# Strassen products in more layers of an attention-and-MoE kernel, under an order fixed in advance

## The chip, the cores and the metric

The kernel runs on one core of a Trainium2 chip. The metric is the device time of one execution in microseconds (us), as a median over runs. The profile is one further look at one execution; its span is some 2 us shorter than that execution's time.

**Work** of TensorE is the number of its matmuls times the time of one in an undisturbed sequence: 215.9 ns for 512 columns, 109 ns for 256, 56 ns for 128, 30.2 ns for 65. **Lag** at a moment is the time since the start of the span minus the work done until then, so a rise of the lag is time that TensorE lost, whether it stood still or ran at a lower clock. A **group** is the tokens of one batch (512 of 576; the other 64 of each batch are gathered in group "r").

## The reference

```python
# q, k, v: (8 batches, 8 heads, 576 tokens, 64); w_in: (512, 2048); w_out: (2048, 512)
r = lambda x: np.maximum(x, 0.0)
phi = lambda x: concat([r(x) * cos_w, r(x) * sin_w])      # cos_w, sin_w by position
kv  = einsum('bhsf,bhsd->bhfd', phi(k), v);  z = sum(phi(k), axis=2)
x   = einsum('bhsf,bhfd->bhsd', phi(q), kv) / (einsum('bhsf,bhf->bhs', phi(q), z) + 1e-6)
h   = tokens_by_512(x) @ w_in                              # "layer 1", 4608 tokens
out = (h * cos(h)) @ w_out                                 # "layer 2"
```

## The kernel before

The kernel makes a list of operations, each with engines that may do it, durations, dependencies and buffer slots. A list scheduler (`Plan.run`) places them in time; the resulting order is then the program of each engine. At run time each engine goes through its part in that order: in a_w_nox, one of the runs below, ScalarE stood 5.30 us before a feature whose data were late, and TensorE waited 4.0 us for a copy that comes behind it.

```python
class Plan:
    def run(self, cold=0.0):
        ...
            t0, e0 = min((c[0], c[1]) for c in cand)       # the engine that can start earliest
            t, _, us, o, _ = min(
                (c for c in cand if c[1] == e0 and c[0] <= t0 + self.EPS),
                key=lambda c: (c[4] if e0 == "DMA" else 0.0, c[3].prio, c[0]))
        ...
```

Loads of q, k and v are issued by SyncE. From batch 2 on, q features pass through a DMA transpose (`qT`), and from batch 3 on x does too (`xT`); SyncE issues these as well, in the same stream. The transfers of the weights are issued by GpSimd; they turn 32 bits into 16 on the way (the eight pieces land as 512 KB each, while the 36.74 MB that the page counts as read from HBM hold q, k and v with 28.3 MB and the weights with 8.4 MB, which is 32 bits a number).

```python
    def load(b, name, half, hs=ALLH):
        ...
            nc.sync.dma_start(out=blocks(m, n)[:, hs], in_=five[:, hs])
        ...
    def q_trans_dma(b, t):
        nc.sync.dma_start_transpose(
            out=qT(b, t), in_=qps[b][:, t].rearrange("p h g d -> p (h g d)"))

    def moe1(key, g, js, cs, s0, s1):                      # plain layer 1
        x = xR if g == "r" else xts[g]
        ...
                nc.tensor.matmul(
                    ps[key][:, n, :], lhsT=w_in_sb[:, c, j * P:(j + 1) * P],
                    rhs=x[:, c, s0:s1], ...)

    NG = 4
    def weights(n):                                        # 0..3 are quarters of w_in, 4..7 of w_out
        g = n % NG
        ...
                    def issue(...):                        # a load of batch 1 waits for w_out piece 1
                        if first:
                            nc.gpsimd.tensor_copy(
                                out=raw[name][0:2, 0, 0, 0:1],
                                in_=w_out_sb[0:2, (NG - 3) * NJT // NG, 0:1])
                        load(b, name, half, hs)
```

All first layers are plain matmuls. The second layer is plain in group 0 and a Strassen product (7 of 8 block products, with sums of blocks by VectorE) in the other groups.

Of the kernel before, what the change touches and what calls it, by code (L numbers as in the profile page):

```python
# [14 lines left out]

class Slot:


    def __init__(self, ring, n=1):
        self.ring, self.left, self.end = ring, n, 0.0  # L20


def flat(x):
    return tuple(z for y in x for z in flat(y)) if isinstance(x, tuple) else (x,)


class Op:
    def __init__(self, alts, prio, fn, deps, lat, acq, rel, at):
        self.alts, self.prio, self.fn, self.deps, self.lat = alts, flat(prio), fn, deps, lat
        self.acq, self.rel, self.at, self.end = acq, rel, at, None  # L30


class Plan:


    SEM, EPS = 0.08, 0.1

    def __init__(self, rings):
        self.ops, self.free = [], {r: [0.0] * n for r, n in rings.items()}
# [6 lines left out]
    def run(self, cold=0.0):  # L46
        users, wait = {}, {}
        for o in self.ops:
            wait[o] = len(o.deps)
            for d in o.deps:  # L50
                users.setdefault(d, []).append(o)
        ready = [o for o in self.ops if not wait[o]]
        clock, order = {}, []
        while ready:
            cand = []
            for o in ready:
                t = max([o.at] + [d.end + d.lat for d in o.deps])
                if any(not self.free[s.ring] for s in o.acq):
                    continue
                for s in o.acq:  # L60
                    t = max(t, min(self.free[s.ring]))
                for e, us in o.alts.items():
                    cand.append((max(t, clock.get(e, 0.0)), e, us, o, t))
            if not cand:
                left = [(o.prio, o.alts, [s.ring for s in o.acq if not self.free[s.ring]],
                         [(d.prio, d.alts) for d in o.deps if d.end is None][:3])
                        for o in self.ops if o.end is None]
                raise RuntimeError("no operation can start: " + repr(left[:12]))
            t0, e0 = min((c[0], c[1]) for c in cand)
            t, _, us, o, _ = min(  # L70
                (c for c in cand if c[1] == e0 and c[0] <= t0 + self.EPS),
                key=lambda c: (c[4] if e0 == "DMA" else 0.0, c[3].prio, c[0]))
            if e0 == "PE" and t < cold:
                us *= 1.7
            for s in o.acq:
                self.free[s.ring].remove(min(self.free[s.ring]))
            o.end = t + us + (self.SEM if us else 0.0)
            clock[e0] = t + us
            for s in o.rel:
                s.left, s.end = s.left - 1, max(s.end, o.end)  # L80
                if not s.left:
                    self.free[s.ring].append(s.end)
            order.append((t, len(order), o, e0))
            ready.remove(o)
            for u in users.get(o, ()):
                wait[u] -= 1
                if not wait[u]:
                    ready.append(u)
        assert len(order) == len(self.ops)
        order.sort(key=lambda x: x[:2])  # L90
        return [(o, e) for _, _, o, e in order]
# [3 lines left out]
def kernel(  # L95
# [50 lines left out]
    WT = cpool.tile([P, 4, HJ, HM], F16, name="WT")  # L146
# [4 lines left out]
    kvzs, kps, qps, qTs, qTr, x16s, xts, gts, sms, osts, ps = ({} for _ in range(11))  # L151
    T, T1 = range(NT), range(NT + 1)
    HS = [slice(0, HB), slice(HB, H)]
    RING = {"m1": 4, "l2": 2, "at": 1}
# [20 lines left out]
    def feat(eng, b, name, t, g, hs=ALLH):  # L175
        dst = (kps if name == "k" else qps)[b][:, t, hs, g, :]
        src, sc = raw[name][:, hs, t, :], CS[:, b % 2, g, t:t + 1]
        if eng == "A":
            nc.scalar.activation(out=dst, in_=src, func=AF.Relu, scale=sc)  # L179
        else:  # L180
            (nc.vector if eng == "V" else nc.gpsimd).tensor_scalar(  # L181
                out=dst, in0=src, scalar1=0.0, scalar2=sc, op0=ALU.max, op1=ALU.mult)
# [10 lines left out]
    def q_tiles(b):  # L193
        qps[b] = apool.tile([P, NT + 1, H, 2, D], F16, name=f"qp{b}", tag="qp", bufs=1)

    def qT_tiles(b):
        qTs[b] = apool.tile([P, NT, H, P], F16, name=f"qT{b}", tag="qT", bufs=1)

    def qR_tiles(b):
        qTr[b] = apool.tile([P, H, P], F16, name=f"qR{b}", tag="qR", bufs=2)  # L200

    def qT(b, t):
        return qTs[b][:, t] if t < NT else qTr[b]
# [27 lines left out]

    def ratio(b, t, tile_, hbs):
        nb, h0 = len(hbs), hbs[0] * HB
        den = apool.tile([P, nb, HB], F32, name=f"den{b}_{t}", tag="den")
        nc.vector.tensor_scalar_add(out=den, in0=tile_[:, :, :, D], scalar1=1e-6)
        rec = apool.tile([P, nb, HB], F32, name=f"rec{b}_{t}", tag="rec")
        nc.vector.reciprocal(out=rec, in_=den)  # L237
        if hbs[0] == 0:
            x16s[(b, t)] = apool.tile([P, H, D], F16, name=f"x16{b}_{t}", tag="x16", bufs=4)
# [19 lines left out]

    def transposes(key, tag, srcs_, **kw):  # L260
# [4 lines left out]
    def q_src(b, t, h):  # L265
        return qps[b][:, t, h].rearrange("p g d -> p (g d)")

    def q_trans_dma(b, t):
        nc.sync.dma_start_transpose(  # L269
            out=qT(b, t), in_=qps[b][:, t].rearrange("p h g d -> p (h g d)"))  # L270
# [12 lines left out]

    def sin(key):
        ps[("ch", key)] = apool.tile([P, SM], F32, name="ch", tag="ch", bufs=4)
# [4 lines left out]
    def gate(key, dst):  # L290
        m = ps[key]
        nc.vector.tensor_tensor(  # L292
            out=dst, in0=m, in1=ps[("ch", key)].rearrange("p (j s) -> p j s", s=m.shape[2]),
            op=ALU.mult)
# [4 lines left out]
    def s_tiles(g):  # L299
        sms[g] = gpool.tile([P, 2, HJ, HT], F16, name=f"s{g}", tag="s")  # L300

    def sums(g, c, n):
# [3 lines left out]
        a12, s1, s2 = gv[:, 1, js, 0:HT], sms[g][:, 0, js], sms[g][:, 1, js]  # L306
        out, in0, in1, op = ((s1, a21, a22, ALU.add), (s2, s1, a11, ALU.subtract),
                             (a21, a11, a21, ALU.subtract), (a12, a12, s2, ALU.subtract))[n]
        nc.vector.tensor_tensor(out=out, in0=in0, in1=in1, op=op)  # L309

    def weight_sum(n):
        wv = w_out_sb.rearrange("p (j e) m -> p e j m", e=2)
        b11, b12 = wv[:, 0, :, 0:HM], wv[:, 0, :, HM:Dm]
        b21, b22 = wv[:, 1, :, 0:HM], wv[:, 1, :, HM:Dm]
        x, y = ((b12, b11), (b22, WT[:, 0]), (b22, b12), (b21, WT[:, 1]))[n]
        nc.vector.tensor_tensor(out=WT[:, n], in0=x, in1=y, op=ALU.subtract)

    def prod(g, n, c):
        gv = gts[g].rearrange("p (j e) s -> p e j s", e=2)
        sv, wv = sms[g], w_out_sb.rearrange("p (j e) m -> p e j m", e=2)  # L320
        lo, hi, ml, mh = slice(0, HT), slice(HT, SM), slice(0, HM), slice(HM, Dm)
        bank, first, lhs, rhs = (
            ("X", True, gv[:, 0, :, lo], wv[:, 0, :, ml]),
            ("Y", True, sv[:, 1], WT[:, 1]),
            ("X", False, gv[:, 1, :, lo], wv[:, 1, :, ml]),
            ("Y", False, gv[:, 0, :, hi], WT[:, 2]),
            ("Z", True, sv[:, 0], WT[:, 0]),
# [469 lines left out]
```

## Time and profile before

| | before |
|---|---|
| median time when the change was predicted | 303.42 us (302.2 to 306.28, 3 runs) |
| span of the profile | 298.7 us |
| work of TensorE, dummies of the start included | 270.1 us |
| mean granted clock | 0.99 |
| lag at 20, 70, 200 us | 8.9, 12.9, 23.5 us |
| tail after the last matmul | 4.7 us |

These lines of the page of the kernel before are the busy time of each engine, the busy tenths in 40 slices of 7.5 us (the clock row in tenths of full speed), and the engines' shares of the chain of work that ended last.

```profile
PE 280.1 (94%) x2565; PEld 201.3 (67%) x2565; DVE 233.7 (78%) x450; ACT 175.6 (59%) x303; POOL 102.0 (34%) x107
PE   8879999899969987999979999999999999999993
DVE  1878888899995798887869798987786786768661
PEclk9979999999999999999999999999999999999998
DMA  7799995897899999999999999715202100200213
PE 55%; DMA 16%; DVE 10%; POOL 5%; SPq 5%; ACT 4%; issue 3%; ACTq 0%; DVEq 0%
```

TensorE bounds the kernel. From 203 us to 292 us it has no gap, and the DMA row has fallen off by then. Earlier, DMA is near full, and here TensorE has its stops. The view of what TensorE waited for (total us, times, longest) begins so; the timeline of TensorE has the longest stop in the middle, at 89.91 us (start, duration, engine, operation, and in brackets the idle time and what ended it).

```profile
PE N L228 <- DVE x L241: 2.8, 2, 2.1
PE M L279 <- ACT xT L159: 2.6, 1, 2.6
PE PY L337 <- DVE s L309: 2.2, 2, 1.6
```

```profile
89.91 3.61 PE L279 MATMUL M<-xT,w_in_sb 128*128 128x512 f16 x16 [2.60 <-ACT xT L159]
```

From 13 us on, when the real work begins, no stop lasts longer than 2.6 us.

### The profile page before, as it was taken

What the parts mean: (1) busy time and instruction counts of PE and PEld (TensorE: products, weight loads), DVE (VectorE), ACT (ScalarE), POOL (GpSimd) and SP (SyncE); (2) the same over time, 40 slices, a digit from 0 to 9 for tenths busy, and PEclk for the clock granted to TensorE, in tenths of its full rate; (3) what the DMA queues carried; (4) which work ended last, traced back from release to release, by engine and by line L of the source; (5) the groups of instructions that cost most, each with busy time, mean ns of one, the idle gap of its engine ahead of it and who ended that gap; (6) DMA issues with size and microseconds to landing.
All of it is one profiled execution on the core that took longest, in us unless ns stands there. A gap on an engine that the chain in (4) does not pass through costs nothing.

```text
span 298.7 us, 6583 instructions
## 1 busy us (share of the span) xinstructions
PE 280.1 (94%) x2565; PEld 201.3 (67%) x2565; DVE 233.7 (78%) x450; ACT 175.6 (59%) x303; POOL 102.0 (34%) x107
## 2 busy tenths in 40 slices
PE   8879999899969987999979999999999999999993
PEld 8768856688855555566646666776666666566782
DVE  1878888899995798887869798987786786768661
ACT  2846748599379797679489497634433443443210
POOL 1370004396191686287077194011002001100500
PEclk9979999999999999999999999999999999999998
DMA  7799995897899999999999999715202100200213
GB/s 218 264 163 203 204 362 183 279 308 120 273 274 235 356 232 169 283 278 203 322 256 202 238 369 195 141 47 151 35 0 94 48 1 32 111 2 0 91 52 140
DMA packets 77086, 53.29 MB, mean 178 GB/s; under 512 B 46080, under 2 KB 74752, under 8 KB 77056
## 3 DMA queue, kind: packets, MB, share of 16 engines
q1 hardware_dynamic: 69760, 39.73, 55.2%
q0 software_dynamic: 6848, 12.59, 16.6%
q10 hardware_dynamic: 448, 0.57, 0.5%
q8 instruction: 20, 0.33, 0.5%
q14 instruction: 10, 0.08, 0.1%
HBM read 36.74 MB, written 9.44 MB: 155 GB/s over the span
## 4 chain that ended last, share of the span: by engine, by line
PE 55%; DMA 16%; DVE 10%; POOL 5%; SPq 5%; ACT 4%; issue 3%; ACTq 0%; DVEq 0%
PE M L279 26%; DMA vm<-in_v_dram 13%; PE PY L337 8%; PE PZ L337 6%; PE PX L337 5%; PE M L376 5%; POOL qp L181 4%; DMA qm<-in_q_dram 3%; PE KV L219 2%; DVE g L292 2%; SPq L171 2%; DVE x L241 2%; PE TP L263 2%; DVE s L309 2%; SPq L269 1%
## 5 line engine op out<-in xcount | busy, mean ns | idle before, releaser
L279 PE MATMUL M<-xT,w_in_sb 128*128 128x512 f16 (+1 forms) x640 | 120.2, 336 | 2.9 <-ACT xT L159 2.6
L286 ACT ACTIVATE ch<-M 128x512 f32<-128x512 f32 x144 | 84.9, 595 | 60.8 <-PE M L279 58.7
L292 DVE TENSOR_TENSOR g<-M,ch 128x512 f16<-128x512 f32 x128 | 85.8, 687 | 27.0 <-ACT ch L286 26.1
L279 PEld LDWEIGHTS <-w_in_sb 128*128 128x128 f16 x704 | 67.3, 98 | 46.6 <-issue 3.1
L181 POOL TENSOR_SCALAR qp<-qm,CS 128x512 f16<-128x512 f32 x29 | 60.0, 2074 | 31.0 <-DMA qm<-in_q_dram 27.0
L337 PEld LDWEIGHTS <-g 128*128 128x128 f16 x560 | 54.1, 98 | 11.5
L369 POOL DMA_DIRECT2D out_dram<-ost x14 | 7.8, 558 | 98.6 <-DVE ost L351 42.5
L179 ACT ACTIVATE kp<-km,CS 128x512 f16<-128x512 f32 x52 | 35.1, 715 | 0.2
L179 ACT ACTIVATE qp<-qm,CS 128x512 f16<-128x512 f32 x40 | 26.9, 713 | 11.9 <-DMA qm<-in_q_dram 11.9
L337 PE MATMUL PX<-w_out_sb,g 128*128 128x256 f16 x224 | 27.6, 273 | 0.0
L241 DVE TENSOR_TENSOR x<-N,rec 128x512 f16<-128x512 f32 (+1 forms) x44 | 26.1, 594 | 1.7 <-DVE rec L237 0.2
L337 PE MATMUL PY<-WT,g 128*128 128x256 f16 x224 | 27.2, 273 | 0.0
L337 PEld LDWEIGHTS <-s 128*128 128x128 f16 x224 | 21.4, 98 | 7.1 <-DVE s L309 2.8
L161 POOL CAST V<-vm 128x512 f16<-128x512 f32 (+1 forms) x22 | 13.9, 664 | 15.9 <-DMA vm<-in_v_dram 15.9
L228 PE MATMUL N<-kvz,qT 128*128 128x65 f16 x256 | 14.7, 196 | 2.3 <-DVE x L241 2.1
L228 PEld LDWEIGHTS <-qT 128*128 128x128 f16 x256 | 12.6, 100 | 6.1 <-issue 3.5
L337 PE MATMUL PY<-WT,s 128*128 128x256 f16 x112 | 14.1, 273 | 2.2 <-DVE s L309 2.2
L181 DVE TENSOR_SCALAR kp<-km,CS 128x512 f16<-128x512 f32 x28 | 15.5, 590 | 0.3 <-DMA km<-in_k_dram 0.2
L292 DVE TENSOR_TENSOR gr<-M,ch 128x512 f16<-128x512 f32 x16 | 10.9, 689 | 5.7 <-ACT ch L286 5.5
L219 PE MATMUL KV<-V,kp 128*128 128x65 f16 x320 | 12.9, 196 | 2.5 <-DVE kp L181 0.7
L279 PE MATMUL M<-xR,w_in_sb 128*128 128x512 f16 x64 | 15.1, 379 | 0.0
L219 PEld LDWEIGHTS <-kp 128*128 128x128 f16 x320 | 11.7, 99 | 4.7 <-issue 2.4
(70 smaller groups left out, 287.7 us busy)
## 6 DMA issues: line engine op xcount, KB each, us to landing
out_dram<-ost POOLq DMA_DIRECT2D x28, 256.0 KB, 4.1
qm<-in_q_dram SPq DMA_DIRECT2D x8, 640.0 KB, 5.3
km<-in_k_dram SPq DMA_DIRECT2D x8, 640.0 KB, 7.0
qm<-in_q_dram SPq DMA_DIRECT2D x8, 512.0 KB, 5.8
km<-in_k_dram SPq DMA_DIRECT2D x8, 512.0 KB, 8.8
vm<-in_v_dram SPq DMA_DIRECT2D x6, 640.0 KB, 8.1
vm<-in_v_dram SPq DMA_DIRECT2D x6, 512.0 KB, 8.9
w_in_sb<-in_moe_w_in_dram POOLq DMA_DIRECT2D x4, 512.0 KB, 9.0
```

Of the source, the lines that this page charges most:

```text
L161: (nc.vector if eng == "V" else nc.gpsimd).tensor_copy(out=out, in_=in_)
L179: nc.scalar.activation(out=dst, in_=src, func=AF.Relu, scale=sc)
L181: (nc.vector if eng == "V" else nc.gpsimd).tensor_scalar(out=dst, in0=src, scalar1=0.0, scalar2=sc, op0=ALU.max, op1=ALU.mult)
L219: nc.tensor.matmul(tile_[:, n, hh, :], lhsT=kps[b][:, t, h].rearrange("p g d -> p (g d)"), rhs=V1[:, t, h, :], start=(t == 0), stop=(t == NT))
L228: nc.tensor.matmul(tile_[:, n, hh, :], lhsT=qT(p, t)[:, h, :], rhs=kvzs[p][:, h, :], start=(i == 0), stop=(i == len(parts) - 1))
L241: nc.vector.tensor_tensor(out=dst, in0=tile_[:, :, :, 0:D], in1=rec.unsqueeze(3).broadcast_to((P, nb, HB, D)), op=ALU.mult)
L279: nc.tensor.matmul(ps[key][:, n, :], lhsT=w_in_sb[:, c, j * P:(j + 1) * P], rhs=x[:, c, s0:s1], start=(c == 0 and n == 0), stop=(c == NCT ...
L286: nc.scalar.activation(out=ps[("ch", key)], in_=ps[key].rearrange("p j s -> p (j s)"), func=AF.Sin, bias=math.pi / 2.0, scale=1.0)
L292: nc.vector.tensor_tensor(out=dst, in0=m, in1=ps[("ch", key)].rearrange("p (j s) -> p j s", s=m.shape[2]), op=ALU.mult)
L337: nc.tensor.matmul(ps[(g, bank)][:, i, :], lhsT=lhs[:, j, i * P:(i + 1) * P], rhs=rhs[:, j], start=(first and i == 0 and j == 0), stop=(j ...
L369: e0.dma_start(out=five[:, t0:t0 + 2, :], in_=blocks(ost, n))
L376: nc.tensor.matmul(ps[("M2", t)], lhsT=gts[0][:, j, t * P:(t + 1) * P], rhs=w_out_sb[:, j, :], start=(j == 0), stop=(j == NJT - 1))
```

## The change

The intent is to save TensorE time with more Strassen products, and to win back the gaps of the middle with an order that was searched instead of scheduled greedily. Strassen is added in the second layer of group 0 and in the first layer of groups 6, r and 7: each takes 112 matmuls of 256 columns (12.2 us) in place of 64 of 512 (13.8 us). The order is a list of operation numbers with their engines. The operations in the text of the kernel still carry the durations of a model, in which loads and transposes form one queue and each lands a fixed 2.0 us (`LAND`) after it. The list scheduler of before uses the same kind of model. Buffers are smaller to make room for the sums of w_in. The weights' pieces go out as 0, 1, 5, 2, 4, 3, 7, 6 instead of 0 to 7, as the order says.

```diff
-    def run(self, cold=0.0):
-        ... (the list scheduler)
+    def run(self):
+        return [(self.ops[int(x.rstrip("VAG"))], x.lstrip("0123456789"))
+                for x in ORDER.split()]
+
+ORDER = """
+22 180 184 883 24 229 25 230 115 818 342 21 40V 41V 42A 60 44V 43A 46V 61A 62 47V 48A 66 63V 34A
+32V 39V 70 33A 31V 53G 54A 51V 30A 52G 38V 50G 35V 37A 36V 45A 49V 71 4G 64 72V 5G 55A 57V 75
+58A 68 76V 7G 56A 77V 85 59A 86V 15G 78 65A 87V 73 9G 74V 227 67A 95 90 96V 88 91V 13G 97V 79A
+92V 11G 80 98 69A 89V 93 105 19G 81V 82V 94A 116 99A 17G 106V 107V 83 100 120 84V 108 110 101V
 ... (72 more such lines; 5G to 19G are the weights' pieces)
-    WT = cpool.tile([P, 4, HJ, HM], F16, name="WT")
+    WT = cpool.tile([P, 3, HJ, HM], F16, name="WT")
+    WS = cpool.tile([P, 3, 2, HJ, P], F16, name="WS")
-    RING = {"m1": 4, "l2": 2, "at": 1}
+    RING = {"m1": 4, "l2": 2, "at": 1, "raw_k": 1, "raw_q": 1, "raw_v": 1, "kp": 1, "qp": 4,
+            "V1": 1, "kvz": 3, "qT": 4, "qR": 2, "xT": 2, "x16": 3, "ch": 3, "g": 2, "s": 3,
+            "ld": 16, "p5": 3, "xs": 1, "ost0": 1, "ost1": 1}
-        qps[b] = apool.tile([P, NT + 1, H, 2, D], F16, name=f"qp{b}", tag="qp", bufs=1)
+        qps[(b, t)] = apool.tile([P, H, 2, D], F16, name=f"qp{b}_{t}", tag="qp", bufs=RING["qp"])
+    def quad(g, qd, n):                                    # one Strassen product of layer 1
+        ...
+        bank, first, lhs, rhs = (
+            ("X", True, a11, x_block(g, 0, 0)), ("Z", True, ws[0], xs[0]),
+            ("Y", False, ws[1], xs[1]), ("X", False, a12, x_block(g, 1, 0)),
+            ("Y", False, s3, x_block(g, 0, 1)), ("Z", False, ws[2], x_block(g, 1, 1)),
+            ("Y", False, a22, xs[2]))[n]
+        ...
+    STR = {6, "r", 7}
 ...
-    def layer2_plain(base):
 ...
+    layer2(0, lambda i: (1, 1, i))                         # group 0's second layer: Strassen as well
 ...
         for o, e in plan.run():
-            if o.fn is not None:
-                o.fn(e) if e in ("A", "V", "G") else o.fn()
+            o.fn(e) if e else o.fn()
```

## The prediction

> **What bounds the kernel now.** TensorE. The page gives PE busy for 280 of 298.7 us, VectorE 78%, ScalarE 59%, GpSimd 34%, clock 0.99. [...] In the timeline, 4 matmuls of 512 columns follow each other in 0.865 us (216 ns each), 8 of 256 columns in 0.87 us (109 ns), 40 KV matmuls in 1.21 us, 8 numerator matmuls in 0.26 us. Times the counts this is about 264 us, besides the dummies of the start. Real work runs from 13.1 us to 294.0 us, so about 19 us of that stretch is lost: some 6 us before 23 us, 1-2 us near 55 us, 2.6 us at 87 us, 3 us at 110-115 us, 2.1 us at 152 us. From 203 us to 292 us TensorE has no gap at all; attention and its DMAs (DMA near full from 60 to 190 us in the slices) are over by then.
>
> **What the change does.** Group 0's second layer and the first layers of groups 6, r and 7 become Strassen: 112 matmuls of 109 ns for 64 of 216 ns, 12.2 for 13.8 us, so 1.6 us less each and 6.4 us in all. The weight loads (98 ns) still fit under 109 ns; second-layer Strassen shows that rate already. Two cover matmuls add 0.4 us. Of these 6 us, 4.8 us lie in the gap-free last stretch and count in full.
>
> The price is VectorE and ScalarE work. Per Strassen first layer: 8 additions (0.60 us apart when back to back) and 4 input sums; ScalarE 8 copies. The second layer gives back 2-3 VectorE adds per group: the first product seeds a PSUM bank. Counted in program order with the trace's durations, the last three groups hold 8.4-9.1 us VectorE and 4-7 us ScalarE work per 10 us of PE: tight, still under PE. The first 60 us of PE work, however, hold 64 us of VectorE work (57 before): sums of group 0 and of both weight matrices. There VectorE bounds: nothing gained, perhaps 1-3 us lost, before about 75 us.
>
> The middle is where the searched order may pay: some 8-9 us of PE gaps after 85 us come from late transposes, V loads and x copies. [...] a sum takes 0.68 us, up to 1.12 us; a K feature 0.48 us, up to 0.90 us. The change gives GpSimd 36 instead of 29 features[...]. I expect half of the middle gaps to go (4-5 us), as DMA stays full there. The tail (last matmul to end, 4.7 us) shortens by about 0.7 us.
>
> **Sum.** 298.7 - 6 (PE work) - 4.5 (gaps) - 0.7 (tail) + 1 (early VectorE) = about 288.5 us of span; the timed median lay 4.7 us above the profiled span before, of which I keep 2: 290.5 us. Range 283 to 298 us. Faster by over 2%: 0.85; within 2%: 0.13; slower: 0.02.
>
> **What would show it.** PE work 6 us less; the gap-free last stretch about 5 us shorter, without waits over 1 us; VectorE share up from 78% to 85-88%, ScalarE to about 66%; VectorE near 100% before 75 us; the chain of waits with more VectorE, less DMA.
>
> **What would make it wrong.** Strassen's alternating chain (copy, add, gate per quad) leaving PE waiting in the last groups, as VectorE is near 90%; or DMA-bound attention ending no earlier than 200 us, so only the last 5 us appear. Or the order removes nearly all gaps: about 282 us.

A matmul record of 512 columns (layer 1 from `xT`) lasts 379 ns in the mean in the kernel before, but in an undisturbed sequence the next one starts after 216 ns. The sum came to 288.5 us of span and 290.5 us of time.

## The result and the profile after

The changed kernel takes 319.6 us (318.79 to 320.27, 4 runs) beside 304.85 us (302.2 to 306.61, 4 runs) of the kernel before. It is slower by a ratio of 1.049, with a 95% interval of 1.0396 to 1.0585. Here and below, a ratio is the mean time of one kernel's fast runs over that of the kernel before in the same rounds, so it isn't quite the ratio of the medians quoted. Executions over 1.5% slower than the fastest of the same kernel are left out of the means. The profiled spans, 317.4 and 298.7 us, differ by more (18.7 us), because the profiled run of before was a fast one of its kind.

The page of the changed kernel, the lines that answer to those above:

```profile
PE 281.4 (89%) x2759; PEld 221.2 (70%) x2759; DVE 247.1 (78%) x465; ACT 194.1 (61%) x355; POOL 122.7 (39%) x121
PE   7779838977978997999899869999999999999993
DVE  1877956978978687688877957899889888798881
PEclk9989987999999999899999989999999999999998
DMA  7699992199997999399999979954502100110203
PE 50%; DMA 28%; DVE 6%; POOL 5%; ACT 4%; SPq 3%; issue 3%; ACTq 0%; DVEq 0%; POOLq 0%
```

TensorE's busy share fell from 94% to 89%, the DMA share of the chain rose from 16% to 28%, and the slices show a hole: slice 6 in PE, slices 6 and 7 in the clock, and slices 7 and 8 in DMA itself. (Slices are counted from 1; each is 7.9 us here.) The waits of TensorE begin now with a DMA, and the timeline has one stop of 5.15 us:

```profile
PE PX L436 <- DMA w_out_sb<-in_moe_w_out_dram: 5.2, 1, 5.2
PE M L325 <- DMA xT<-x: 4.2, 2, 2.7
PE N L262 <- ACT kvz L195: 2.7, 2, 1.6
PE M L325 <- ACT qp L215: 2.4, 1, 2.4
```

```profile
45.78 1.86 PE L436 MATMUL PX<-w_out_sb,g 128*128 128x256 f16 x8 [5.15 <-DMA w_out_sb<-in_moe_w_out_dram]
```

The work of TensorE is 264.0 us, 6.1 us less than before. Lag tells where the time went, by stretch of the span:

| lag, us | before | after | after loses more by |
|---|---|---|---|
| at 70 us | 12.9 | 24.9 | 12.0 |
| from 70 to 200 us | +10.6 | +19.5 | 8.9 |
| from 200 us to the last matmul | +0.4 | +4.2 | 3.8 |
| sum at the last matmul | 23.9 | 48.6 | 24.7 |

The sum fits: 24.7 us of lag more, less 6.1 us of work, are 18.6 of the 18.7 us of span. The last row but one is 23.9 - 23.5 and 48.6 - 44.4; a tail of 4.7 and 4.8 us comes after it.

A part of this is clock. The trace of the changed kernel has stretches at half clock from 20.9 us (3.4 us), 44.8 us (6.8 us), 126.7 us (3.4 us) and 188.1 us (3.4 us), 17.0 us in all beside 3.4 us before. TensorE did 7.8 us of work in them (1.4 us before). At half clock, matmuls of 256 columns start 213 ns apart in the median, beside 109 ns else, so each us of work there takes about one more us, and about 6.4 us of the 24.7 us go there. All these stretches last 3.41 or 6.83 us, and in the 3.41 us before the one at 44.8 us there is no matmul at all. What sets them off is not shown. (The list at the end has two stretches that came after shorter stops.) Windows of the trace (us busy on each engine, count, then clock, DMA share, GB/s), four us each around the stop:

```profile
44.00:48.00 4.00, 1.86 (x8) 1.14 (x8) 2.17 (x4) 0.32 (x1) 0.00 (x0) 0.59 1.09 364
48.00:52.00 4.00, 3.67 (x20) 2.71 (x20) 3.23 (x5) 1.04 (x3) 3.22 (x6) 0.55 0.34 112
```

In the second window TensorE is busy for 3.67 us, but makes only 20 matmuls of 256 columns, which is 2.2 us of work.

The cause of the stop itself can be read from SyncE's timeline: the first loads of batch 1, before and after.

```profile
33.88 0.60 SPq L171 DMA_DIRECT2D qm<-in_q_dram  x1
34.53 0.63 SPq L173 DMA_DIRECT2D qm<-in_q_dram  x1
35.28 0.96 SPq L171 DMA_DIRECT2D km<-in_k_dram  x1
```

```profile
27.42 0.60 SPq L207 DMA_DIRECT2D qm<-in_q_dram  x1
28.06 0.64 SPq L209 DMA_DIRECT2D qm<-in_q_dram  x1
28.80 0.60 SPq L207 DMA_DIRECT2D km<-in_k_dram  x1
29.45 4.88 SPq L209 DMA_DIRECT2D km<-in_k_dram  x1
34.43 4.50 SPq L207 DMA_DIRECT2D vm<-in_v_dram  x1
```

Batch 1's loads are held until piece 1 of w_out (number 5) has landed. Piece 5 now goes out third instead of sixth, so they start 6.5 us earlier, with five pieces issued behind that one instead of two; two of the issues then take 4.9 and 4.5 us, where one takes 0.6 us otherwise. The last piece of w_out landed at 45.8 us instead of 38.8 us. From issue to landing, min, median and max of w_out's pieces, before and after:

```profile
DMA to landing us min/median/max: 13.3/16.4/19.3
```

```profile
DMA to landing us min/median/max: 10.0/17.5/25.0
```

After 52 us there is nothing left to move for 8 us, and batch 2's q load goes out at 64.0 us instead of 51.4 us. That delay of 12.6 us does not simply stay: by batch 3 the q load is 7.9 us behind that of before and by batch 4 9.8 us, then 17.4 us at batch 5 and 22.5 us at batch 7. So there are two losses, one before batch 2 and one from batch 4 on.

### The profile page after: what moved, and what is told of

The parts are those of the page before. It is cut to its first block, busy times and chain, and to the rows that moved or that the text cites. A ratio compares the mean times of both kernels' runs of the same rounds, so it can differ in the third digit from the quotient of the medians.

```text
span 317.4 us, 7064 instructions
## 1 busy us (share of the span) xinstructions
PE 281.4 (89%) x2759; PEld 221.2 (70%) x2759; DVE 247.1 (78%) x465; ACT 194.1 (61%) x355; POOL 122.7 (39%) x121
## 4 chain that ended last, share of the span: by engine, by line
PE 50%; DMA 28%; DVE 6%; POOL 5%; ACT 4%; SPq 3%; issue 3%; ACTq 0%; DVEq 0%; POOLq 0%
PE M L325 11%; PE SD L436 9%; DMA km<-in_k_dram 9%; DMA w_out_sb<-in_moe_w_out_dram 9%; PE PZ L436 7%; PE PX L436 7%; DMA vm<-in_v_dram 6%; PE M L381 5%; PE SD L381 3%; PE YZ L381 3%; DMA qT<-qp 2%; POOL kp L217 2%; SPq L207 2%; PE PY L436 1%; PE KV L253 1%
## 5 line engine op out<-in xcount | busy, mean ns | idle before, releaser
L325 PE MATMUL M<-xT,w_in_sb 128*128 128x256 f16 (+1 forms) x512 | 94.4, 332 | 10.9 <-DMA xT<-x 4.2
L387 ACT ACTIVATE ch<-M 128x512 f32<-128x512 f32 x116 | 67.8, 595 | 45.4 <-PE M L325 30.3
L338 DVE TENSOR_TENSOR g<-M,ch 128x512 f16<-128x512 f32 x110 | 73.0, 685 | 16.7 <-ACT ch L387 15.9
L436 PEld LDWEIGHTS <-g 128*128 128x128 f16 x640 | 63.2, 100 | 22.1 <-issue 10.1
L217 POOL TENSOR_SCALAR qp<-qm,CS 128x512 f16<-128x512 f32 x19 | 39.8, 2100 | 34.0 <-DMA qm<-in_q_dram 32.3
L217 POOL TENSOR_SCALAR kp<-km,CS 128x512 f16<-128x512 f32 x17 | 38.5, 2271 | 9.6 <-DMA km<-in_k_dram 9.6
L215 ACT ACTIVATE qp<-qm,CS 128x512 f16<-128x512 f32 x43 | 29.6, 713 | 10.7 <-DMA qm<-in_q_dram 8.6
L215 ACT ACTIVATE kp<-km,CS 128x512 f16<-128x512 f32 x38 | 25.5, 713 | 3.7 <-DMA km<-in_k_dram 3.7
L381 PEld LDWEIGHTS <-w_in_sb 128*128 128x128 f16 x192 | 18.7, 98 | 2.9 <-issue 0.4
L436 PE MATMUL PZ<-w_out_sb,g 128*128 128x256 f16 x128 | 16.6, 273 | 0.5 <-DVE PZ L338 0.5
L217 DVE TENSOR_SCALAR kp<-km,CS 128x512 f16<-128x512 f32 x25 | 13.4, 568 | 4.5 <-DMA km<-in_k_dram 4.5
L436 PE MATMUL PZ<-WT,s 128*128 128x256 f16 x128 | 16.3, 273 | 0.0
L381 PEld LDWEIGHTS <-WS 128*128 128x128 f16 x144 | 14.0, 98 | 3.0 <-issue 1.2
L436 PE MATMUL SD<-WT,g 128*128 128x256 f16 x112 | 15.4, 283 | 0.6 <-ACT ost L195 0.6
## 6 DMA issues: line engine op xcount, KB each, us to landing
w_in_sb<-in_moe_w_in_dram POOLq DMA_DIRECT2D x4, 512.0 KB, 10.1
```

The lines of the kernel that those rows point to most:

```text
L215: nc.scalar.activation(out=dst, in_=src, func=AF.Relu, scale=sc)
L217: (nc.vector if eng == "V" else nc.gpsimd).tensor_scalar(out=dst, in0=src, scalar1=0.0, scalar2=sc, op0=ALU.max, op1=ALU.mult)
L325: nc.tensor.matmul(ps[key][:, n, :], lhsT=w_in_sb[:, c, j * P:(j + 1) * P], rhs=x[:, c, s0:s1], start=(c == 0 and n == 0), stop=(c == NCT ...
L338: (nc.vector if eng == "V" else nc.gpsimd).tensor_tensor(out=out, in0=in0, in1=in1, op=op)
L381: nc.tensor.matmul(ps[(g, qd, bank)][:, i, :], lhsT=lhs[:, c, 2 * qd + i, :], rhs=rhs[:, c, :], start=(first and i == 0 and c == 0), stop= ...
L387: nc.scalar.activation(out=ps[("ch", key)], in_=ps[key].rearrange("p j s -> p (j s)"), func=AF.Sin, bias=math.pi / 2.0, scale=1.0)
```

## The experiments

Eighteen kernels ran, in six jobs, each with three rounds beside the kernel before. The medians of before in these jobs are 304.11, 302.16, 304.07, 303.88, 303.1 and 302.63 us, on five different chips; so across jobs, differences of about 1% in a ratio, or 2 us, are not to be leaned on. "Old order of weights" below means pieces 0 to 7 in turn in the changed kernel. A kernel that is wrong is named so.

### Job 1: the start, and who made the order

**a_worder**: the changed kernel with the old order of weights. The tokens 15G, 9G, 11G, 19G, 17G become 9G, 11G, 15G, 17G, 19G (pieces 0 to 3 are 5G to 11G, pieces 4 to 7 are 13G to 19G); nothing else moves.

```diff
-58A 68 76V 7G 56A 77V 85 59A 86V 15G 78 65A 87V 73 9G 74V 227 67A 95 90 96V 88 91V 13G 97V 79A
-92V 11G 80 98 69A 89V 93 105 19G 81V 82V 94A 116 99A 17G 106V 107V 83 100 120 84V 108 110 101V
+58A 68 76V 7G 56A 77V 85 59A 86V 9G 78 65A 87V 73 11G 74V 227 67A 95 90 96V 88 91V 13G 97V 79A
+92V 15G 80 98 69A 89V 93 105 17G 81V 82V 94A 116 99A 19G 106V 107V 83 100 120 84V 108 110 101V
```

> Edit: the changed kernel with the eight weight transfers issued in the old order (four of w_in, then four of w_out), nothing else. Theory W (weights): the new order issues the second w_out piece third; the loads of batch 1, which wait for that piece, then start at 27.4 us instead of 33.9 us and take DMA time from the other weights, so that the last w_out piece lands at 45.8 us instead of 38.8 us; TensorE stops 5 us, its clock halves for 6.8 us, and everything of batch 2 comes some 12 us later. It expects w_out landed by 39-41 us, no TensorE stop over 1.5 us there, loads of batch 2 at 52-58 us instead of 64 us, and 304 to 312 us instead of 319.6. Rival V (VectorE overloaded before 75 us, as the prediction had it): the work of VectorE is the same, so 317 to 321 us and batch 2 as late as before.

Measured: 314.38 us, ratio 1.0323 (1.0244 to 1.0402), span 310.4 us. The long stop is gone, and the last piece takes at most 19.6 us to land. The gain is 5.2 us in the medians and 7.0 us in the span; the time missed the range that was expected, so the weights' order is a part of the loss and not most of it.

The lag at 70 us says the same: 21.2 us, beside 24.9 us in the changed kernel and 12.9 us before. Of the 12.0 us that were lost there, 3.7 us are back and 8.3 us are not. Where half of the rest lies can be read from TensorE's timeline. In the Strassen products of group 0's second layer there are five stops, 4.2 us in sum: on a piece of w_out, on a sum of w_out's blocks (`WT`), on a gated value (`g`), and on a copy and an addition between two products.

```profile
34.18 0.81 PE L436 MATMUL PX<-w_out_sb,g 128*128 128x256 f16 x6 [0.89 <-DMA w_out_sb<-in_moe_w_out_dram]
35.75 1.03 PE L436 MATMUL PY<-WT,s 128*128 128x256 f16 x8 [0.76 <-DVE WT L416]
42.07 0.83 PE L436 MATMUL PX<-w_out_sb,g 128*128 128x256 f16 x6 [1.36 <-DVE g L338]
43.59 1.91 PE L436 MATMUL PX<-w_out_sb,g 128*128 128x256 f16 x16 [0.69 <-ACT p L195]
49.53 1.03 PE L436 MATMUL PZ<-w_out_sb,g 128*128 128x256 f16 x8 [0.53 <-DVE PZ L338]
```

In the kernel before, whose second layer of group 0 is plain, the same view shows no stop from 28 to 55 us. No run undoes the Strassen product of group 0 alone, so this is read from traces and not tested.

**a_gate**: the new order of weights, but batch 1's loads wait for the piece of w_out with the last number, 7. (In the new order this is the last but one to be sent; piece 6 lands 2.5 us after it.)

```diff
-                                in_=w_out_sb[0:2, (NG - 3) * NJT // NG, 0:1])
+                                in_=w_out_sb[0:2, (NG - 1) * NJT // NG, 0:1])
```

> Edit: the changed kernel with its own weight order, but batch 1's loads wait for the last w_out piece instead of the second. Theory W, if the overlap of the two is what costs: w_out all landed by 38-40 us, batch 1's loads at 39-40 us and landed near 52-54 us, TensorE stop under 2 us, 308 to 315 us. If the order of the pieces itself were the cause and not the overlap: the fourth w_in piece still late, w_out late, 318 to 321 us. Rival V: 317 to 321 us.

Measured: 312.07 us, ratio 1.0252 (1.0175 to 1.033, so whether it is over 2% slower than before is unclear), span 310.5 us. With the new order of pieces kept, keeping the loads away from them gives back 7.5 us. The stop on w_out falls from 5.2 to 1.1 us. The lag at 70 us is 20.5 us. So it is the overlap of loads and weights that costs, not the order of the pieces as such.

**b_worder**: the kernel before, with the new order of the pieces (but for the last two, which are not swapped) and nothing else.

```diff
     def weights(n):
+        n = (0, 1, 5, 2, 4, 3, 6, 7)[n]
         g = n % NG
```

> Edit: the kernel before with the weights in the new order (w_in, w_in, w_out piece 2, w_in, w_out, w_in, w_out, w_out), nothing else. Theory W: batch 1's loads start near 27-28 us, the last w_out piece lands near 44-46 us, TensorE stops 3 to 6 us in the second layer of group 0, and the time grows by 4 to 12 us to 308 to 316 us. Rival V: no change over 1%, 303 to 307 us.

Measured: 312.25 us, ratio 1.0254 (1.0169 to 1.0339), span 310.9 us, 12.2 us longer than before. One line turns the old kernel into one that is 8 us slower. Its stop lies on w_in, since plain layer 1 needs those pieces when w_out's have overtaken them, and half clock follows it (from 33.4 us for 6.8 us). The wait of weight loads (PEld) in the trace:

```profile
PEld L279 <- DMA w_in_sb<-in_moe_w_in_dram: 7.6, 2, 5.2
```

**a_greedy**: all operations of the changed kernel, but ordered by the list scheduler of before instead of the fixed text.

```diff
-        return [(self.ops[int(x.rstrip("VAG"))], x.lstrip("0123456789"))
-                for x in ORDER.split()]
+        users, wait = {}, {}
+        ... (the list scheduler of the kernel before, with one line more for the engine name "Vp")
```

> Edit: all operations of the changed kernel (Strassen in the same layers, same buffers), ordered by the list scheduler of the kernel before in place of the fixed searched order. Theory W: the scheduler issues the weights in their plain order, so no late w_out; 295 to 308 us, clearly faster than the searched order. If the operations themselves (more VectorE and ScalarE work, chains of the Strassen quads) are the cause: 316 us or more.

Measured: 325.35 us, ratio 1.0682 (1.0584 to 1.0781). As a whole the searched order is better than greedy for these operations, so the theory that the order alone is the culprit was wrong. By stretches it is both better and worse. From 70 to 200 us the lag of a_greedy grows by 11.3 us, near the 10.6 us of before, where it grows by 19.5 us in the changed kernel and by 16.1 us in a_worder. After 200 us a_greedy loses 21.3 us, where the changed kernel loses 4.2 us. Its leading wait is that of TensorE on VectorE's additions between the products of a second layer (3.7 us in four stops).

### Job 2: buffers, VectorE, and the operations without layer 1

**a_w_alias** (wrong): a control with the old order of weights, in which the three sums of w_in share one buffer to make room.

```diff
-    WS = cpool.tile([P, 3, 2, HJ, P], F16, name="WS")
+    WS1 = cpool.tile([P, 2, HJ, P], F16, name="WS")
```

> Control for the next run, wrong result on purpose: the changed kernel with the old weight order, and the three Strassen sums of w_in share one buffer, which frees 8 KB per partition and leaves it unused. No work is added or taken away. Both theories: 311 to 316 us, as the run with the old weight order (314.4).

**a_w_alias_rings** (wrong): the same, with the room given to larger rings.

```diff
-"qp": 4, ... "x16": 3, "ch": 3
+"qp": 6, ... "x16": 4, "ch": 4
```

> As the control, and the freed 8 KB are given back to the buffers that the change had cut: query features 6 instead of 4, x tiles 4 instead of 3, sine tiles 4 instead of 3. Theory B (buffers): with 4 query feature tiles ScalarE and GpSimd wait in order for a transpose to land before the fifth tile, the sines behind it wait too, TensorE stops (2.4 us at 121 us), and the raw query buffer is freed late, so each next load comes late; this expects the spacing of the KV groups of batches 2 to 7 to fall from 25 us towards 23 us, and the time to fall by 3 to 9 us against the control. Rival O (the fixed order itself, whose queue positions were chosen for other times): under 1% of change.

Measured: 314.75 us (ratio 1.0448) for the control and 313.02 us (1.0395) with the rings. Larger rings give 1.7 us, or 0.5%. The q load of batch 5 still went out at 130.5 us. The smaller buffers are not where the loss lies.

**a_w_nosum0** (wrong): the old order of weights, without the VectorE sums of group 0's second layer.

```diff
     def sums(e, g, c, n):
+        if g == 0:
+            return
```

(The products of group 0 that used the sums then read the gated values instead.)

> Wrong result on purpose: the changed kernel with the old weight order, without the eight Strassen sums of group 0's second layer on VectorE (about 5.4 us of work); its products read the gated tiles instead, so TensorE's work stays. Theory V (VectorE is what bounds before 75 us): 3 to 6 us less than 314.4, TensorE's lost time between 30 and 80 us down from 11.6 to 6-8 us. If the chain of loads and features of batch 1 bounds there instead: under 1.5 us less.

Measured: 312.93 us (ratio 1.0376), 1.8 us under the control of this job and 1.5 us under a_worder of job 1. The lag at 70 us is 21.6 us, beside 21.2 us in a_worder: taking the sums away did not help before 70 us, though VectorE is busy for 21.1 us instead of 27.3 us of the 30 us from 30 to 60 us. So the amount of VectorE's work is not what bounds the start. That TensorE waits for single results of VectorE there (three of the five stops above) is another matter; this run keeps those stops.

**a_greedy_nostr**: the list scheduler, and no Strassen in layer 1.

```diff
-    STR = {6, "r", 7}
+    STR = set()
```

> The changed kernel under the old list scheduler (325.4 us) with plain first layers in all groups: Strassen of layer 1 alone is undone, the other parts of the change (Strassen in group 0's second layer, seeded banks, smaller buffers, features on GpSimd) stay. If Strassen in layer 1 costs more than it saves under that scheduler (its stalls after 210 us): 308 to 316 us. If the rest of the change is the cause: 322 us or more. Against the kernel before (304.1 us) what remains is what the rest of the change costs under one and the same scheduler.

Measured: 319.99 us, one of the four runs slow (ratio 1.0588, 1.0514 to 1.0662). Against a_greedy, Strassen in layer 1 costs 5.4 us in the medians under the list scheduler instead of saving 4.8; by the ratios of the two jobs it is 2.9 us, and their intervals overlap, so a cost is not shown, only that nothing is saved. The rest of the change (group 0's Strassen, features spread over engines, other rings), with the order that the scheduler makes of it, takes 17.8 us more than the old operations under the same scheduler. Operations and order are not taken apart by this: from 70 to 200 us this kernel's lag grows by 20.9 us, that of a_greedy by 11.3 us. Three stops on transposes of x lead its waits; the longest is 6.6 us:

```profile
PE M L297 <- DMA xT<-x: 9.5, 3, 6.6
```

### Job 3: no loads

**a_w_noload** and **b_noload** (wrong): the changed kernel with the old order of weights, and the kernel before, each without the loads of batches 2 to 7; features are made of batch 1's data.

```diff
     def load(b, name, half, hs=ALLH):
+        if b >= 2:
+            return
```

> Wrong result on purpose: the changed kernel with the old weight order, and the loads of q, k and v of batches 2 to 7 left out, so features are made again from the data of batch 1. All work of the compute engines and all transposes stay. Theory I (input pipeline: what is left of the loss is that each next load waits for the last feature of the batch before and that its data come later than the fixed order allows for): the TensorE time lost between 60 and 200 us falls from 20 us to under 8 us, the time falls by 15 us or more, to 290 to 300 us, and comes out below the same cut of the kernel before, by the 4 to 6 us of TensorE work that Strassen takes away. Rival O (the added VectorE and ScalarE work and the fixed order of the compute engines hold TensorE up themselves): 304 us or more, and still above the same cut of the kernel before.

> Wrong result on purpose: the kernel before with the loads of batches 2 to 7 left out. Theory I: it gains less than the changed kernel does, since its input pipeline was matched to its order: 290 to 299 us. Rival O: no prediction of its own for this kernel, but it stays below the same cut of the changed kernel.

Measured: 297.59 us (ratio 0.9831, 0.974 to 0.9923) and 297.84 us (0.9751, 0.9616 to 0.9885). The loads cost the changed kernel 16.8 us of its 314.38 and the kernel before 6.2 us of its 304.07 (by the ratios 15 and 7.6 us). In the medians the two are level without loads; but two of b_noload's four runs are slow, and by the fast runs alone the changed kernel stays 0.8% (2.4 us) above it, with overlapping intervals. So loads make most of the remaining difference between the two: 7.4 of 9.8 us by the ratios. The middle is good then: between 70 and 200 us the changed kernel's lag grows by 3.7 us (19.2 to 22.9) and that of before by 5.0 us (15.2 to 20.2). The 6.1 us of work that the change saves are used up: it loses 4.0 us more by 70 us, 1.3 us less up to 200 us, and 3.3 us more after that (22.9 to 26.4 at 290 us, beside 20.2 to 20.4). That it would still be ahead by 4 to 6 us was expected and missed. The traces also differ by clock: that of b_noload has 10.2 us at half clock before 70 us, which cost it 4.6 us, that of a_w_noload none. So the 4.0 us by 70 us are rather too low than too high.

Transposes of x, from issue to landing, in the kernel with the old order of weights and in the same one without loads:

```profile
DMA to landing us min/median/max: 2.4/4.1/12.2
```

```profile
DMA to landing us min/median/max: 2.4/2.6/4.3
```

### Job 4: data or traffic, and the clock

**a_w_ghost** (wrong): the loads are made, but nobody reads them, and they wait for nobody: features of batches 2 to 7 come from a constant tile.

```diff
-        src, sc = raw[name][:, hs, t, :], CS[:, b % 2, g, t:t + 1]
+        src = raw[name][:, hs, t, :] if b < 2 else GH[:, hs, 0, :]
+        sc = CS[:, b % 2, g, t:t + 1]
```

(V is copied from the constant tile as well, and the sums of w_in share one buffer as in a_w_alias.)

> Wrong result on purpose: the changed kernel with the old weight order and the shared buffer of the control; the loads of batches 2 to 7 are all made, but features and V casts of these batches read a constant tile, so no load waits for a feature and no feature for a load. The DMA traffic is that of the full kernel, only the waits between loads and features are gone. Rival T (traffic: the loads slow the transposes and the weights down by sharing the DMA engines): stays at 308 to 315 us. Theory I (the chain load, last feature, next load through one buffer each): near the run without loads, 296 to 302 us.

Measured: 311.07 us (307.03 to 314.25, the last of them slow), ratio 1.0297. The waits of the features for their data are gone, yet only 3.3 us of the 16.8 us are back (in the ratio 0.3% against a_worder and 1.5% against the control, from other jobs, so 3 us is not sharp). The loads go out nearly when they did: the q loads at most 3.2 us earlier than in a_worder. So most of the cost of the loads is that they are moved, not that they are waited for. The transposes land as late as with the real loads (at most 11.4 us), and TensorE stops where it stopped before:

```profile
119.51 1.89 PE L328 MATMUL M<-xT,w_in_sb 128*128 128x512 f16 x8 [3.33 <-ACT qp L217]
149.56 1.02 PE L328 MATMUL M<-xT,w_in_sb 128*128 128x512 f16 x4 [2.48 <-DMA xT<-x]
176.86 1.04 PE L328 MATMUL M<-xT,w_in_sb 128*128 128x512 f16 x4 [2.12 <-DMA xT<-x]
```

The first of the three also leads to a transpose: in a_worder's stop at the same place, ScalarE's `qp` had itself waited 1.7 us for a `qT` transpose to free its buffer.

**a_warm**: the changed kernel itself (right result), with 85 dummy matmuls of 128 columns where TensorE waits for w_out.

```diff
+        if g == 0 and n == 0 and c == 1:
+            dummies("at", 85)
```

> The changed kernel itself (new weight order) with 85 small dummy matmuls (about 4.8 us) on TensorE in the place where it stands still for 5.2 us for the last w_out piece, so that its clock should not drop. If the halved clock after the stop is a cost of its own: no half-clock stretch at 45 to 52 us and 2 to 3.5 us less than 319.6. If what follows there is held by the inputs of batch 1 and by the copies of group 0 anyway: within 1 us.

Measured: 314.98 us (313.9 to 316.0), ratio 1.039, beside 319.6 us without. So 4.6 us are won in the medians with matmuls that compute nothing; by the ratios of the two jobs it is 3.0 us, and their intervals overlap. Half clock falls from 17.0 us to 3.4 us in this trace. The two windows around the stop now read:

```profile
44.00:48.00 4.00, 2.91 (x29) 2.38 (x27) 3.18 (x5) 1.21 (x2) 0.56 (x1) 1.00 1.03 353
48.00:52.00 4.00, 3.91 (x44) 3.49 (x43) 3.79 (x6) 3.38 (x6) 4.00 (x7) 1.00 0.06 19
```

From 48 to 52 us there are 44 matmuls instead of 20. The stretches at 126.7 and 188.1 us are gone as well; that the dummies did that is not shown, since a stop of 2.37 us was followed by half clock in the changed kernel and one of 2.60 us in the kernel before was not. Without the dummies, TensorE's work is ahead of the changed kernel's by 3.0 us at 60 us and at 120 us (1.2 to 4.3 us between), and by 5.9 us at 130 us. So about 3 us are what filling the stop won; the rest came with the later stretches.

### Job 5: another queue for the loads, and both repairs of the start

**a_w_pload** and **b_pload**: the loads of batches 2 to 7 are issued by GpSimd instead of SyncE, in the changed kernel with the old order of weights and in the kernel before.

```diff
-            nc.sync.dma_start(out=blocks(m, n)[:, hs], in_=five[:, hs])
+            e = nc.gpsimd if b >= 2 else nc.sync
+            e.dma_start(out=blocks(m, n)[:, hs], in_=five[:, hs])
```

> After's order with the old weight order, but the loads of batches 2 to 7 are issued by GpSimd on its own queue instead of SyncE on the queue of the transposes; same loads, same waits for buffers, right result. Compared with the run with the old weight order alone (314.4 us). Theory Q (the transposes are late because they stand behind loads on the same queue and in the same issuing engine): transposes of x land in about 3 us in the middle and below 7 us at worst (12.2 there), single issues of SyncE stay below 2.7 us (5.5 there), and the time falls by 6 to 12 us to 302-308 us. Theory E (loads and transposes share the DMA engines whatever queue they come from): late transposes as there (worst over 9 us), time within 3 us of 314. GpSimd that waits in its own order for buffers may delay its features: then a loss, with PE waits on GpSimd features.

> The same edit of the kernel before: loads of batches 2 to 7 issued by GpSimd. Theory Q: 0 to 5 us faster than before (its loads cost at most 6.2 us in all). Theory E: within 2 us of before. A loss of several us would show that GpSimd, waiting for a buffer, holds up its own features.

Measured: 325.2 us (ratio 1.0718, 1.0679 to 1.0757) and 312.19 us (307.49 to 319.08; its two fast runs give 1.016; it isn't compared closely). The transposes are not faster when no load stands in their queue; the slowest landed after 16.1 us. The issues section of a_worder, then of a_w_pload (operation, count, median us from issue to landing), and a stretch of SyncE's timeline of a_w_pload:

```profile
xT<-x SPq DMA_TRANSPOSE x20, 4.1
```

```profile
xT<-x SPq DMA_TRANSPOSE x20, 5.1
```

```profile
105.12 10.09 SPq L687 DMA_TRANSPOSE xT<-x  x2
```

Two issues, of 4.9 and 4.4 us, hold SyncE for 10 us although no load is in its stream. Theory Q falls. Of theory E the late transposes came true; its time, within 3 us of 314, was missed. The median landing is 5.1 us with the loads on another queue and 4.1 us with them on the same one, and the page of a_w_pload counts the packets of both queues over the same 16 DMA engines (36.7% and 32.2% of their span). That it became 11 us slower is not a clean measurement of the queue, though: GpSimd spends 0.7 us on each issue. In the trace a feature waited on GpSimd for 10.7 us, and the V load of batch 4 stood behind it.

**a_worder_gate**: both repairs of the start. **a_wg_pload**: both, and the loads on GpSimd.

```diff
-                                in_=w_out_sb[0:2, (NG - 3) * NJT // NG, 0:1])
+                                in_=w_out_sb[0:2, (NG - 1) * NJT // NG, 0:1])
```

> The changed kernel with both repairs of its start: weights in the old order and batch 1's loads behind the last piece of w_out. Alone they gave 5.2 and 7.5 us. If both repair the same overlap: 309-312 us, with no PE wait on w_out over 1 us. If they are independent: 304-307 us.

> Both repairs of the start and the loads on GpSimd's queue, the best that I can build of the changed kernel. Theory Q: 298-305 us, about level with before. Theory E: 308-312 us as with the two repairs alone.

Measured: 315.29 us (ratio 1.0408, 1.0382 to 1.0434) and 326.43 us (319.67 to 332.1, ratio 1.0623). Two repairs are no better than one: they mend the same overlap. Both together delay batch 1, whose loads go out at 41.4 us (34.5 us in a_worder, 37.3 us in a_gate), and the lag at 70 us is 24.4 us. Its half clock is 10.2 us. The last kernel is as slow as a_w_pload; no cause is read from it.

### Job 6: no wait for x

Why does the kernel before bear the same loads better? Its transposes of x land no sooner: median 5.5 and at most 10.1 us, beside 4.1 and 10.8 us in the changed kernel. But the programs differ in the lead. Between the last numerator of a batch and the first matmul that reads that batch's x, TensorE has this much other work (counted in program order with the matmul times above):

| batch | 3 | 4 | 5 | 6 | 7 |
|---|---|---|---|---|---|
| before, us | 4.0 | 12.2 | 18.9 | 27.0 | 56.9 |
| after, us | 5.7 | 6.1 | 8.9 | 10.4 | 36.3 |
| a_greedy, us | 5.7 | 5.8 | 11.8 | 12.1 | 36.2 |

**a_w_nox** and **b_nox** (wrong): in groups 2 to 5, layer 1 reads w_in itself in the place of x. Transposes and loads are made as ever.

```diff
-        x = xR if g == "r" else xts[g]
+        x = xR if g == "r" else w_in_sb if g in (2, 3, 4, 5) else xts[g]
```

> Wrong result on purpose. The changed kernel with the old weight order, in which the first layers of groups 2 to 5 read a constant tile (w_in itself) instead of the group's x, so TensorE never waits there for the transposes of x; the transposes and loads are made as before. In the programs, TensorE has 12.2, 18.9 and 27.0 us of matmul work between the last numerator of batches 4, 5 and 6 and the first matmul that reads that batch's x in the kernel before, and only 6.1, 8.9 and 10.4 us in the changed one, while a transpose of x may land 12 us after its issue. Theory L (the changed order has too little lead, so late transposes stop TensorE where they don't in the kernel before): the stops at 153 and 180 us go, and TensorE loses 4 to 6 us less between 60 and 200 us: 308-311 us against 314.4. Rival C (the stops only pass the delay of the chain loads, features, q transposes, numerators on; without them TensorE waits for that chain a little later): within 2 us of 314.4.

> Wrong result on purpose, the control: the same edit of the kernel before. Theory L: its lead already covers most transposes, so it gains little, 0 to 2.5 us (some 2 us at 87 us and 110 us wait for transposes of x in groups 2 and 3): 301-304 us. If it gains as much as the changed kernel, the lead is not what sets the two apart.

Measured: 311.84 us (ratio 1.0313, 1.0254 to 1.0371) and 303.05 us (1.0028, 0.9964 to 1.0092). The control is as expected: before gains nothing, so transposes of x that land late cost it nothing in these groups. In the changed kernel the stops at 121, 153 and 180 us are gone, and at 180 us its lag is 30.2 us where a_worder has 35.6 us. But the time is only 2.5 us less, and the ratio hardly lower. Most is given back in one stop at 189.71 us. TensorE waits there for a copy by ScalarE; and ScalarE waits for batch 7's q load, because a q feature comes ahead of that copy in its order. First the wait of TensorE, then the timeline of ScalarE:

```profile
PE PX L436 <- ACT SD L195: 4.0, 1, 4.0
```

```profile
187.90 0.72 ACT L215 ACTIVATE qp<-qm,CS 128x512 f16<-128x512 f32 x1 [5.30 <-DMA qm<-in_q_dram]
188.53 0.58 ACT L387 ACTIVATE ch<-M 128x512 f32<-128x512 f32 x1
189.00 0.17 ACT L270 ACTIVATE den<-N 128x8 f32<-128x8 f32 x1
189.06 0.60 ACT L195 ACTIVATE SD<-PX 128x512 f32<-128x512 f32 x1
```

So both theories are half right. The short lead makes TensorE stop (theory L), and behind it the next chain, loads to features, is as tight (rival C). The last row of the table limits theory L further: a_greedy has leads almost as short, and its transposes of x take up to 9.1 us, yet from 70 to 200 us it has one stop on them, of 1.7 us, and loses little more than the kernel before. A short lead exposes TensorE to late transposes; it is not enough to explain the loss of the middle. With either the waits for x or those for the data of loads taken away alone (a_w_nox, a_w_ghost), 2 to 4 us come back; with the traffic taken away, 16.8 us.

## Why the prediction was wrong

The prediction's span was 288.5 us and 317.4 us were measured, 28.9 us more. By stretches the miss is 11.0 us at the start (12.0 instead of 1), 13.4 us in the middle (8.9 lost instead of 4.5 won), 3.8 us after 200 us and 0.8 us in the tail; the work was 0.1 us better than predicted. So two steps failed above all, "+ 1 (early VectorE)" and "- 4.5 (gaps)".

**Right: the work.** TensorE's work fell by 6.1 us as predicted ("6 (PE work)"), as the counts of matmuls in the trace give it. VectorE and ScalarE did get more to do, 247.1 us and 194.1 us; their shares, predicted as 85 to 88% and 66%, stayed at 78% and 61% of a longer span.

**Wrong, the largest loss: the start, "+ 1 (early VectorE)".** It was 12.0 us at 70 us of the span. The prediction costed VectorE's sums and did not cost the weights' new order and the gate that hangs on piece 5. What took its place, in part: batch 1's loads start 6.5 us earlier and run beside five weight pieces, the last of which lands 7 us later; TensorE stops for 5.15 us (0.97 us more on w_in) and is at half clock for 6.8 us from 44.8 us on. Shown by a_gate (7.5 us back with one number changed), a_worder (5.2 us), b_worder (8 us lost in the old kernel), and a_warm (about 3 us back by keeping TensorE busy in the stop). These overlap and may not be added. "There VectorE bounds" fell with a_w_nosum0. With the overlap mended, 8.3 us (a_worder) or 7.6 us (a_gate) of the 12.0 us by 70 us stay. Of these, 4.2 us are the five stops in a_worder's trace in group 0's second layer, which the prediction costed as 1.6 us won: its products wait for a piece of w_out (0.9 of the 4.2 us), for gated values, copies, additions and sums of blocks, where the plain layer of before has no stop. This is read, not tested. The last 4 us or so have no explanation; the loads of later batches are about 2 us of them (19.2 us of lag at 70 us without them).

**Wrong: "I expect half of the middle gaps to go (4-5 us), as DMA stays full there".** The stretch from 70 to 200 us lost 8.9 us more than before instead of 4 to 5 less. That DMA was full was taken for what keeps the other half of the gaps; it brought new ones. Transposes land later beside loads: without loads a transpose of x lands in 2.6 us in the middle and 4.3 us at most, with them up to 12.2 us. The order leaves 6 to 10 us of work between the numerators of batches 4 to 6 and the use of their x, where the old one leaves 12 to 27 us. Shown: the loads cost 16.8 us in the changed kernel and 6.2 us in the old (the two runs without loads; 15 and 7.6 us by the ratios); the larger part is their traffic and not waiting for their data (a_w_ghost); another queue for them does not make the transposes faster (a_w_pload); and the old kernel gains nothing when the wait for x is taken away (b_nox), where the changed one loses its three stops, but passes most of them on (a_w_nox). Not shown is why the old order bears the same traffic better. A longer lead is one reason that was argued; no order with more lead was built for these operations, and a_greedy, with little more, loses only 11.3 us in this stretch. There the searched order itself is the worse one.

**Wrong: "4.8 us lie in the gap-free last stretch and count in full".** After 200 us the changed kernel loses 3.8 us more than before, so about 1 us of the 4.8 us is left as a net gain there in the trace. The prediction named these chains as a danger: copies and additions between products. They are short waits: nine places, 3.3 us in sum, the longest idle time 0.65 us, and the same nine in a_worder and without loads. So "without waits over 1 us" held; their sum is what was not costed.

**Wrong: the tail, "shortens by about 0.7 us".** It is 4.8 us beside 4.7 us.

**VectorE beside GpSimd.** The durations did not grow in a way that matters: a K feature on VectorE has a mean of 568 ns (590 before), on GpSimd 2271 ns, where a Q feature takes 2100 ns (2074 before). In the trace of before, all 11 K features on VectorE that took over 0.5 us overlapped an operation of GpSimd, and 9 of the other 17 did. Nothing in these runs shows it as a part of the loss.

**Clock.** The prediction gave it as 0.99 and didn't consider that it could fall. By the trace, half clock cost 6.4 us more of TensorE's time than before; this is inside the terms above and not a further one.

No kernel with the right result beats the one before: of the changed ones, a_gate came closest with 312.07 us. Left open are the rest of about 4 us by 70 us, why the old order bears the loads better, and which part of the new operations, or of the order made of them, takes 17.8 us more than the old ones under the same list scheduler (a_greedy_nostr).

## What to carry to other kernels

Before a change of order is costed, list which transfers run at the same time in it, and follow each gate to the transfer that opens it: here one weight piece sent three places earlier opened the next batch's loads into the rest of the weights and cost 5 to 8 us. Compare the lead that an order leaves ahead of each DMA result with the worst landing under load (12 us here, not the 2.6 us of a quiet one); a model with one landing time does not see that. That a longer lead would have won the middle is argued and not shown. A block product that saves 1.6 us of matmuls can cost more in the waits between its products: here 4.2 us in group 0, as read from one trace. A stop of TensorE that couldn't be avoided was cheaper here when it was filled with dummy matmuls: about 3 us were won that way from a stop of 5.15 us.

## What the traces show of issues, landings and half clock

- The issue itself takes time here: for a transpose of x it took SyncE 1.24 us in the median and 5.50 us at most in a_worder, where the median landing was 4.1 us (1.20 us of 2.6 us without loads); and two load issues took 4.88 and 4.50 us instead of 0.6 us in the changed kernel.
- From issue to landing, next to other DMAs, transposes of x took 4.1 us in the median and 12.2 us at most (a_worder), and 2.6 and 4.3 us without loads (a_w_noload).
- Half clock came at 126.7 us and at 188.1 us of the changed kernel, right after stops of only 2.37 and 2.65 us, and in the kernel before a stop of 2.60 us at 89.9 us brought none. In the 3.41 us before these two stretches TensorE is busy for 30% and 27%, but in a_worder half clock followed 3.41 us in which it was 65% busy (from 59.0 us). So the length of a stop alone does not tell whether half clock follows; what does is not shown.
